# A state-space layer beside a gated feed-forward: another product first, parameters as rows, centring on ScalarE

## The chip, the core and the metric

The kernel runs on one NeuronCore of a Trainium2 chip. Its engines are TensorE (PE, matrix products into PSUM), VectorE (DVE), ScalarE (ACT), GpSimd (POOL) and SyncE (SP, whose queue issues most DMAs). Each has its own instruction stream, and they meet through semaphores. The metric is device time in microseconds (us) of one launch. All times in this text are us unless marked otherwise.

## The reference

```python
def _layernorm(x, axis=-1, eps=1e-5):
    m = jnp.mean(x, axis=axis, keepdims=True)
    v = jnp.var(x, axis=axis, keepdims=True)
    return (x - m) / jnp.sqrt(v + eps)

def _A_ref(x, Lambda_re, Lambda_im, B_re, B_im, C_re, C_im, log_dt, Dskip):
    Lam = Lambda_re + 1j * Lambda_im
    dt = jnp.exp(log_dt)
    Lam_bar = jnp.exp(dt * Lam)
    B_bar = ((Lam_bar - 1.0) / Lam)[:, None] * (B_re + 1j * B_im)
    Bu = jnp.einsum("bld,pd->blp", x + 0j, B_bar)
    # h_t = Lam_bar * h_{t-1} + Bu_t, over the 2048 tokens
    ...
    return 2.0 * jnp.einsum("blp,dp->bld", hseq, C_re + 1j * C_im).real + x * Dskip

def _B_ref(x, w_gate, w_up, w_down):
    return (_gelu(x @ w_gate) * (x @ w_up)) @ w_down

xn = _layernorm(x)
out = x + _A_ref(xn, ...) + _B_ref(xn, ...)
```

There are 2048 tokens of 512 features, 512 complex states, and 1376 hidden columns in the feed-forward. All inputs and the output are bf16.

## The kernel before

**Blocks and tiles.** The tokens are cut into four blocks of 512, each of four tiles of 128. For a block the kernel does the layer norm of its tiles (`LN`), turns them so that features lie on the partitions (`TR`, transposing DMAs; in block 0 `TR_lead`, by TensorE), multiplies by B (`BU`: eight results, real and imaginary part of four groups of 128 states, four matmuls each), rotates, scans and rotates back (`CHAIN`, all on VectorE), multiplies by the gate and up weights (`GU`: eleven column tiles of 128 hidden columns, each a gate and an up product of four matmuls), and makes the output (`DN`: eleven matmuls with w_down and eight with C for each token tile). The factor of B_bar is folded into C (`scale_C`), so B is used as it is loaded, by a transposing DMA (`ld_tr`).

**Evictions.** Results of `BU` are copied out of PSUM by ScalarE (L661), two of block 0 by VectorE (L660). `gu_out` takes the gelu of the gate (L715) and a copy of the up product (L717) on ScalarE and multiplies them on VectorE (L719, hmul), through rings of three buffers. PSUM has eight banks; `next_bank` deals them in turn, so a bank is wanted again eight products later.

**Who sets the order.** The operations are listed with estimated durations. `Sched.schedule` keeps TensorE's and SyncE's order as listed. On VectorE, ScalarE and GpSimd it plays the kernel through with its own estimates, always taking the ready operation whose due time (worked back from TensorE's list, less the operation's `slack`) is earliest, and filling gaps with others. `S.pin` fixes the first operations of an engine in the order given. `Sched.emit` then writes each engine's list with its semaphore waits; the order is fixed when the kernel is built, and an engine waits at the head of its list.

**The lead.** SyncE issues the four tiles of x of block 0, B_re and B_im, then the gate and up weights in four chunks of columns each (`FCH`: 256, 384, 384 and 352 columns; x tiles 4 to 7 after the second chunk). ScalarE issues the three parameter vectors (log_dt, Lambda_im, Lambda_re), element by element onto 128 partitions (L465). TensorE first multiplies zeros (L768, 12 matmuls of 512 columns). Tiles 0 to 2 get their mean and variance by bn_stats and bn_aggr on VectorE (L512, L513), tile 3 by sums on ScalarE (`sums`, L517 to L521). The square root is a power on GpSimd (L542; for a whole block L571), the reciprocal and the centring are on VectorE (L544, L527). Each tile is turned by TensorE (L556, four transposes) and copied by ScalarE (L559, "evT"). While tiles come in, TensorE does the B product for tiles 0 and 1 in pieces of 128 columns in four banks; after the last tile it does what is left of the eight B results.

```python
        S.pin(evT0, t1, evT1, t2, evT2, evT3, t3)
        sint, cost, warm, dtab = tables()
        S.pin(*dtab)
        ev = []
        for k in range(8):
            lead_mm((k,), 2 if k < 4 else 0, 4)
            ev.append(bu_out(0, combos[k][0], combos[k][1], k, "scalar" if k < 6 else "vector"))
        S.pin(*ev[0:6], sint, cost, warm)
        S.pin(*ev[6:8])
```

Here t1 and t2 are the exponentials of the parameters (`decay`, L592 and L595), t3 the sine of 16 small columns (L601), sint and cost the sine tables that the rotations need (L611, L612, from fractions that VectorE makes, L605 to L609). `warm` loads the gelu table before the first gelu (L614).

**After the lead** the order on TensorE is: column tiles 0 to 10 of block 0, B product 1, column tiles of block 1, B product 2, output of block 0, column tiles of block 2, B product 3, output of block 1, column tiles of block 3, outputs of blocks 2 and 3. `LN(1)` uses bn_stats on VectorE, `LN(2)` and `LN(3)` use sums on ScalarE and centre on VectorE.

Of the kernel before, what the change touches and what calls it, by code (L numbers as in the profile page):

```python
# [75 lines left out]
class Sched:  # L76
# [58 lines left out]
    def schedule(self):  # L135
# [41 lines left out]
        while nleft:  # L177
            best = None
            for e in ENGINES:
# [29 lines left out]
                if best is None or st < best[0]:  # L209
                    best = (st, op)  # L210
            st, op = best
# [108 lines left out]
D_TINY = 90.0  # L320
def d_act(n, ptr=0): return 100.0 + 0.833 * n + 90.0 * ptr


def build(nc, ins, out):
    with ExitStack() as es:
# [51 lines left out]
        NEGt = [[A.sub(A.sub(NEG_all, "NEG%d" % b, b), "NEG%d_%d" % (b, j), j) for j in range(4)] for b in range(NB)]  # L377
# [14 lines left out]
        RQb, RQt = per_tile("RQ")  # L392
        HALF = A.alloc("HALF", [4], BF16)
# [4 lines left out]
        LDT = A.alloc("LDT", [KP], BF16)  # L398
# [63 lines left out]
        def ld_param(T_, nm, queue="sync"):  # L462
            def f(e):
                with nc.allow_non_contiguous_dma(reason="tiny per-state parameter vectors"):
                    return e.dma_start(T_.ap, ins[nm].rearrange("(s p) -> p s", p=128))  # L465
            return S.dma(f, 1024, writes=[T_], tag="ld_" + nm, queue=queue, issue=530.0, lat=4000.0)

        def ld_tr(dst, nm):
            return S.dma(lambda e: e.dma_start_transpose(dst.ap, ins[nm]), 3.0 * 512 * 1024 * 0.33, writes=[dst], tag="tr_" + nm,
                         issue=1900.0, lat=1000.0)  # L470

        for tt in range(4):
            ld_x(tt, 1)
        S.pin(*[ld_param(T_, nm, "scalar") for T_, nm in ((LDT, "A_log_dt"), (LIM, "A_Lambda_im"), (LRE, "A_Lambda_re"))])
        ld_tr(BBT[0], "A_B_re")
        ld_tr(BBT[1], "A_B_im")
        for ci in range(4):
            ld_w(WG, WGc, ins["B_w_gate"], ci)
            ld_w(WU, WUc, ins["B_w_up"], ci)
            if ci == 1:  # L480
                ld_x(4, 4)

        def late_loads():
            ld_x(8, 4)
# [23 lines left out]
        GATE = {"gelu": [], "last_gelu": None}  # L508

        def stats(tt):  # L510
            b, j = divmod(tt, 4)
            return [V(lambda e: e.bn_stats(ST[tt].ap, X[tt].ap), 640, [X[tt]], [ST[tt]], "bnst"),  # L512
                    V(lambda e: e.bn_aggr(MVt[b][j].ap, ST[tt].ap), 100, [ST[tt]], [MVt[b][j]], "bnag")]  # L513
# [16 lines left out]
        def LN_lead():  # L530
            st = [stats(tt) for tt in range(3)]
            a3 = sums(3)
            S.pin(*a3)
            ve, rq, ln = [], [], []
            for tt in range(4):
                if tt < 3:
                    ve.append(V(lambda e, tt=tt: e.tensor_scalar(VEt[0][tt].ap, MVt[0][tt].ap[:, 1:2], EPS_BF16, None, ALU.add),
                                D_TINY, [MVt[0][tt]], [VEt[0][tt]], "ve"))
                else:
                    ve.append(V(lambda e, tt=tt: e.tensor_scalar(VEt[0][tt].ap, SSQt[0][tt].ap, 1.0 / D, EPS_BF16, ALU.mult, ALU.add),  # L540
                                D_TINY, [SSQt[0][tt]], [VEt[0][tt]], "ve"))
# [3 lines left out]
                ln.append(center(tt, tt == 3))  # L545
            S.pin(*st[0], ve[0], *st[1], ve[1], rq[0], ln[0], *st[2], ve[2], rq[1], ln[1], ve[3], rq[2], ln[2], rq[3], ln[3])

        def TR_lead(tt):
            bank, half = 6 + tt % 2, tt // 2
            part = bank_part(bank, 1024 * half, 1024 * half + 1024)  # L550
            pt = PSH[bank][:, 512 * half:512 * half + 512]

            def f(e):
                ins_ = None
                for dk in range(KD):
                    ins_ = e.transpose(pt[:, 128 * dk:128 * dk + 128], XN[tt].ap[:, 128 * dk:128 * (dk + 1)], IDN.ap)  # L556
                return ins_
            PE(f, 400, [XN[tt], IDN], [part], "T0")
            return ACT(lambda e: e.activation(XNT[0].ap[:, :, 128 * tt:128 * tt + 128],  # L559
                                              pt.rearrange("p (k t) -> p k t", k=KD), ACTF.Copy),  # L560
                       d_act(512), [part], [XNTt[tt]], "evT")

        def LN(b, on_act=True):
            for tt in range(4 * b, 4 * b + 4):
                sums(tt) if on_act else stats(tt)
            if on_act:
                V(lambda e: e.tensor_scalar(VBb[b].ap, SSQb[b].ap, 1.0 / D, None, ALU.mult), D_TINY, [SSQb[b]], [VBb[b]], "vb")
# [313 lines left out]
```

## Time and profile before

| | |
|---|---|
| times of three runs | 184.75, 184.6, 183.53 us; median 184.6 |
| profiled execution: own time, span | 183.76 us, 182.0 us |
| granted TensorE clock, mean | 0.999 |
| busy PE / DVE / ACT / POOL | 174.4 / 163.4 / 95.6 / 9.2 us |
| DMA moved | 12.38 MB |

The span runs from the first to the last instruction of one profiled execution. A busy share is a mean over the whole span. In the chain view each row names what the end waited for at that time; in the timeline each row is a group of like instructions: start, duration, engine, line, operation, and in brackets how long the engine had stood idle and what ended that. "PEld" is a weight load, "SPq" and "ACTq" are DMA issues.

### The profile page before, as it was taken

To read this page: it belongs to the slowest core of one execution; us is meant where nothing else is said; L and a number is where in the kernel's file an instruction comes from. 1 tells how busy PE (TensorE), PEld (TensorE's weight loads), DVE (VectorE), ACT (ScalarE), POOL (GpSimd) and SP (SyncE) were. 2 spreads that over 40 slices of the span, in tenths; PEclk is the share of its full clock that TensorE was granted. 3 is DMA by queue.
4 is the path that set the end of the run, shared out by engine and by line. 5 is a ranking of instruction groups with operands and counts; after the bars stand their busy time and mean duration, and the time that the engine had idled before them with its cause. 6 is when DMAs were issued, how large, how long until landed. Compare 5 with 4: busy or idle time off the path is not lost.

```text
span 182.0 us, 2379 instructions
## 1 busy us (share of the span) xinstructions
PE 174.4 (96%) x848; PEld 83.3 (46%) x863; DVE 163.4 (90%) x269; ACT 95.6 (53%) x184; POOL 9.2 (5%) x13
## 2 busy tenths in 40 slices
PE   7399999999999999999999999999999999999994
PEld 2184444444444444444444444444444444444463
DVE  4799989999999999979999999998999999999431
ACT  2589996899999999600766774000567720000000
POOL 2400320000020000040000000000000000000000
PEclk9999999999999999999999999999999999999999
DMA  4999414997003100002330000001100000002021
GB/s 93 229 273 361 132 29 98 359 237 198 0 0 77 38 4 0 0 0 86 87 63 2 0 0 0 0 4 58 58 0 0 0 4 0 0 29 86 0 88 31
DMA packets 26827, 12.38 MB, mean 68 GB/s; under 512 B 16992, under 2 KB 26816, under 8 KB 26816
## 3 DMA queue, kind: packets, MB, share of 16 engines
q1 hardware_dynamic: 25232, 12.23, 25.8%
q10 hardware_dynamic: 1584, 0.00, 0.5%
q8 instruction: 7, 0.11, 0.3%
q14 instruction: 4, 0.03, 0.1%
HBM read 6.46 MB, written 2.10 MB: 47 GB/s over the span
## 4 chain that ended last, share of the span: by engine, by line
PE 93%; DMA 2%; ACT 2%; issue 1%; SPq 1%; DVE 0%
PE PS L708 42%; PE PS L742 21%; PE PS L652 15%; PE PS L753 15%; DMA arena<-in_A_x_dram 2%; SPq L451 1%; ACT arena L559 1%; ACT arena L521 0%; ACT arena L517 0%; PE PS L556 0%; DVE arena L760 0%; ACT arena L519 0%; ACT arena L592 0%
## 5 line engine op out<-in xcount | busy, mean ns | idle before, releaser
L708 PE MATMUL PS<-arena 128*128 128x512 bf16 (+1 forms) x345 | 76.3, 379 | 0.4
L708 PEld LDWEIGHTS PS<-arena 128*128 128x128 bf16 (+1 forms) x352 | 35.2, 100 | 40.8
L715 ACT ACTIVATE arena<-PS 128x512 bf16<-128x512 f32 (+1 forms) x44 | 26.4, 600 | 34.9 <-PE PS L708 17.2
L742 PE MATMUL PS<-arena 128*128 128x512 bf16 (+3 forms) x184 | 38.9, 366 | 0.2
L690 DVE TENSOR_TENSOR_SCAN arena<-arena 128x512 bf16<-128x512 f32 x32 | 38.8, 1252 | 0.0
L652 PE MATMUL PS<-arena 128*128 128x512 bf16 (+2 forms) x157 | 28.7, 336 | 2.9 <-ACT arena L592 2.5
L717 ACT ACTIVATE arena<-PS 128x512 bf16<-128x512 f32 (+1 forms) x44 | 26.3, 597 | 7.0 <-PE PS L708 7.0
L753 PE MATMUL PS<-arena 128*128 128x512 bf16 (+1 forms) x134 | 28.5, 366 | 0.1
L742 PEld LDWEIGHTS PS<-arena 128*128 128x128 bf16 (+1 forms) x187 | 18.3, 98 | 20.0
L652 PEld LDWEIGHTS PS<-arena 128*128 128x128 bf16 x160 | 14.3, 98 | 16.3 <-DMA arena<-in_A_B_re_dram 2.6
L753 PEld LDWEIGHTS PS<-arena 128*128 128x128 bf16 x136 | 13.2, 97 | 14.4
L719 DVE TENSOR_TENSOR arena<-arena 128x512 bf16<-128x512 bf16 (+1 forms) x44 | 17.8, 417 | 1.8 <-ACT arena L717 1.3
L661 ACT ACTIVATE arena<-PS 128x512 bf16<-128x512 f32 x30 | 17.0, 597 | 2.9 <-PE PS L652 2.9
L679 DVE TENSOR_TENSOR arena<-arena 128x4096 bf16<-128x4096 bf16 x8 | 18.3, 2288 | 0.1
L680 DVE TENSOR_TENSOR arena<-arena 128x4096 bf16<-128x4096 bf16 x8 | 18.3, 2282 | 0.0
L760 DVE TENSOR_TENSOR arena<-PS,arena 128x512 bf16<-128x512 f32 (+1 forms) x17 | 10.9, 652 | 8.0 <-PE PS L753 7.8
L730 DVE TENSOR_TENSOR arena<-arena 128x512 f32<-128x512 bf16 x16 | 10.8, 689 | 0.4
L681 DVE TENSOR_TENSOR arena<-arena 128x2048 bf16<-128x2048 bf16 x8 | 9.8, 1223 | 0.2
L571 POOL TENSOR_TENSOR arena<-arena 128x4 bf16<-128x4 bf16 x3 | 6.0, 2005 | 64.4 <-DVE arena L570 64.4
L517 ACT ACTIVATE arena<-arena 128x512 bf16<-128x512 bf16 x9 | 5.6, 627 | 3.2 <-DMA arena<-in_A_x_dram 3.1
L521 ACT ACTIVATE arena<-arena 128x512 bf16<-128x512 bf16 x9 | 6.5, 717 | 0.1
L729 DVE TENSOR_TENSOR arena<-arena 128x512 bf16<-128x512 bf16 x16 | 6.4, 417 | 0.0
(61 smaller groups left out, 76.3 us busy)
## 6 DMA issues: line engine op xcount, KB each, us to landing
out_dram<-arena SPq DMA_DIRECT2D x15, 128.0 KB, 1.7
arena<-in_A_x_dram SPq DMA_DIRECT2D x3, 512.0 KB, 5.4
arena<-in_B_w_down_dram SPq DMA_DIRECT2D x1, 1280.0 KB, 7.1
arena<-in_B_w_gate_dram SPq DMA_DIRECT2D x2, 384.0 KB, 5.6
arena<-in_B_w_up_dram SPq DMA_DIRECT2D x2, 384.0 KB, 6.1
arena<-in_A_x_dram SPq DMA_DIRECT2D x4, 128.0 KB, 2.9
arena<-in_B_w_gate_dram SPq DMA_DIRECT2D x1, 352.0 KB, 7.7
arena<-in_B_w_up_dram SPq DMA_DIRECT2D x1, 352.0 KB, 7.6
```

The costliest lines, as they stand in the source:

```text
L652: ins_ = e.matmul(PS[bank][:, c0:c1], BBT[c].ap[:, dk, 128 * s:128 * (s + 1)], XNT[b].ap[:, dk, c0:c1], start=(dk == 0), stop=(dk == KD - 1))
L661: return ACT(lambda e: e.activation(ss.ap, PS[bank][:, :], ACTF.Copy), d_act(512), [BANK[bank]], [ss], "evBu")
L679: V(lambda e: e.tensor_tensor(TB.ap, ssb.ap, sin4, ALU.mult), d_dve_tt2x(4096), [ssb, SINT], [TB], tag)
L680: V(lambda e: e.tensor_tensor(TA.ap, ssb.ap, cos4, ALU.mult), d_dve_tt2x(4096), [ssb, COST], [TA], tag)
L690: V(lambda e, g=g, rb=rb, init=init: e.tensor_tensor_scan(g.ap, rb, g.ap, init, ALU.mult, ALU.add), d_dve_scan(512), [g, PA[RRr]] + ([CARc ...
L708: ins_ = e.matmul(PS[bank][0:m, :], W.ap[:, dk, 128 * ft:128 * ft + m], XNT[b].ap[:, dk, :], start=(dk == 0), stop=(dk == KD - 1))
L715: GATE["last_gelu"] = ACT(lambda e: e.activation(GG[kk].ap[0:m, :], PS[bg][0:m, :], ACTF.Gelu_apprx_tanh), d_act(512), [BANK[bg]], [GG[kk] ...
L717: ACT(lambda e: e.activation(UPB[kk].ap[0:m, :], PS[bu][0:m, :], ACTF.Copy), d_act(512), [BANK[bu]], [UPB[kk]], "evU")
L719: V(lambda e: e.tensor_tensor(HTt[k2][ft].ap[0:m, :], GG[kk].ap[0:m, :], UPB[kk].ap[0:m, :], ALU.mult), d_dve_tt2x(512), [GG[kk], UPB[kk]] ...
L742: ins_ = e.matmul(o_, HTt[k2][ft].ap[0:m, tok], WD.ap[0:m, ft, c0:c1], start=(ft == 0), stop=False)
L753: ins_ = e.matmul(o_, SSc[k3][s][c].ap[:, tok], CT[c][s].ap[:, c0:c1], start=False, stop=(s == KP - 1 and c == 1))
L760: V(lambda e, o_=o_, ko=ko: e.tensor_tensor(OUTB[ko].ap[:, c0:c1], o_, XD[ko].ap[:, c0:c1], ALU.add), d_dve_1x(c1 - c0), [part, XD[ko]], [ ...
```

## The change

The order in block 0 becomes: gate and up products of the first three column tiles, in six banks, for token tiles 0 and 1 in pieces of 128 columns, then for tiles 2 and 3 in one piece of 256; then the whole B product of block 0, all eight results copied out by VectorE; then column tiles 3 to 10. The first two gate and up chunks are loaded right behind the four tiles of x, B after them, and x tiles 8 to 11 earlier. The parameters are loaded as four rows of 128 (256 bytes each) and turned by TensorE between two parts of the warm-up (`TR_par`, into PSUM); ScalarE reads them there, and the product dt * Lambda_re becomes the scale of four exponentials. The gelu table is loaded a first time after the exponentials and again after the sine tables; the gelu and the up copy of the third column tile come behind that. Tile 3 gets its statistics on VectorE like the others. Blocks 2 and 3 are centred on ScalarE, with a scale and a bias per token. Some due times get a slack of 4000 ns, the estimate of a transposing load of B or C grows, and the B product goes through the real results first.

```diff
         def ld_param(T_, nm, queue="sync"):
-            def f(e):
-                with nc.allow_non_contiguous_dma(reason="tiny per-state parameter vectors"):
-                    return e.dma_start(T_.ap, ins[nm].rearrange("(s p) -> p s", p=128))
-            return S.dma(f, 1024, writes=[T_], tag="ld_" + nm, queue=queue, issue=530.0, lat=4000.0)
+            return S.dma(lambda e: e.dma_start(T_.ap[0:KP, :], ins[nm].rearrange("(s p) -> s p", p=128)), 1024,
+                         writes=[T_], tag="ld_" + nm, queue=queue, lat=2300.0)
...
+        S.pin(*[ld_param(T_, nm, "scalar") for T_, nm in ((PRM[0], "A_log_dt"), (PRM[1], "A_Lambda_re"), (PRM[2], "A_Lambda_im"))])
         for tt in range(4):
             ld_x(tt, 1)
-        S.pin(*[ld_param(T_, nm, "scalar") for T_, nm in ((LDT, "A_log_dt"), (LIM, "A_Lambda_im"), (LRE, "A_Lambda_re"))])
+        ld_gu(0)
+        ld_gu(1)
         ld_tr(BBT[0], "A_B_re")
         ld_tr(BBT[1], "A_B_im")
-        for ci in range(4):
-            ld_w(WG, WGc, ins["B_w_gate"], ci)
-            ld_w(WU, WUc, ins["B_w_up"], ci)
-            if ci == 1:
-                ld_x(4, 4)
+        ld_x(4, 4)
+        ld_gu(2)
+        ld_gu(3)
+        ld_x(8, 4)
...
         def stats(tt):
             b, j = divmod(tt, 4)
-            return [V(lambda e: e.bn_stats(ST[tt].ap, X[tt].ap), 640, [X[tt]], [ST[tt]], "bnst"),
-                    V(lambda e: e.bn_aggr(MVt[b][j].ap, ST[tt].ap), 100, [ST[tt]], [MVt[b][j]], "bnag")]
+            return [V(lambda e: e.bn_stats(ST[tt].ap, X[tt].ap), 640, [X[tt]], [ST[tt]], "bnst", slack=4000.0),
+                    V(lambda e: e.bn_aggr(MVt[b][j].ap, ST[tt].ap), 100, [ST[tt]], [MVt[b][j]], "bnag", slack=4000.0)]
...
         def LN_lead():
-            st = [stats(tt) for tt in range(3)]
-            a3 = sums(3)
-            S.pin(*a3)
+            st = [stats(tt) for tt in range(4)]
...
-            S.pin(*st[0], ve[0], *st[1], ve[1], rq[0], ln[0], *st[2], ve[2], rq[1], ln[1], ve[3], rq[2], ln[2], rq[3], ln[3])
+            S.pin(*st[0], ve[0], *st[1], ve[1], rq[0], ln[0], *st[2], ve[2], rq[1], ln[1], *st[3], ve[3], rq[2], ln[2])
+            return rq[3], ln[3]
...
+        PPB = (5, 5, 4)
+        PP = [PSH[PPB[i]][:, KP * i:KP * (i + 1)] for i in range(3)]
+
+        def TR_par(i):
+            PE(lambda e: e.transpose(PP[i], PRM[i].ap[0:KP, :], IDN.ap[0:KP, 0:KP]), 100, [PRM[i], IDN], [BANK[PPB[i]]], "Tp")
...
+            if on_act:
+                V(lambda e: e.tensor_tensor(NRQb[b].ap, NEGb[b].ap, RQb[b].ap, ALU.mult), D_TINY, [NEGb[b], RQb[b]], [NRQb[b]], "nrq")
+            for j in range(4):
+                tt = 4 * b + j
+                if on_act:
+                    ACT(lambda e, j=j, tt=tt: e.activation(XN[tt].ap, X[tt].ap, ACTF.Identity, bias=NRQb[b].ap[:, j:j + 1],
+                                                           scale=RQb[b].ap[:, j:j + 1]),
+                        d_act(512, 1), [X[tt], NRQb[b], RQb[b]], [XN[tt]], "ln")
+                else:
+                    center(tt, False)
...
         def decay():
+            exps = [ACT(lambda e: e.activation(DTB.ap, PP[0], ACTF.Exp), 200, [BANK[5]], [DTB], "exp_dt")]
+            for s in range(KP):
+                exps.append(ACT(lambda e, s=s: e.activation(PA[RRr].ap[:, s:s + 1], PP[1][:, s:s + 1], ACTF.Exp,
+                                                            scale=DTB.ap[:, s:s + 1]),
+                                200, [BANK[5], DTB], [A.sub(PA[RRr], "RR_%d" % s, s)], "exp_a"))
+            c = [ACT(lambda e: e.activation(LRE.ap, PP[1], ACTF.Copy), 200, [BANK[5]], [LRE], "par"),
+                 ACT(lambda e: e.activation(LIM.ap, PP[2], ACTF.Copy), 200, [BANK[4]], [LIM], "par")]
...
-        def BU(b):
-            for s in range(KP):
-                for c in range(2):
-                    bank = next_bank()
-                    bu_mm(b, s, c, bank, 0, 512, [XNT[b]])
-                    bu_out(b, s, c, bank)
+        def BU(b, eng="scalar", banks=None):
+            combos = [(s, c) for c in range(2) for s in range(KP)]
+            for i, (s, c) in enumerate(combos):
+                bank = banks[i] if banks else next_bank()
+                bu_mm(b, s, c, bank, 0, 512, [XNT[b]])
+                bu_out(b, s, c, bank, eng)
...
+        def lead_mm(pairs, t0, t1):
+            for k in pairs:
+                gu_mm(0, k, 2 * k, 2 * k + 1, t0, t1)
+
+        def preload(tag):
+            return ACT(lambda e: e.activation(DUM.ap[:, 1:2], DUM.ap[:, 0:1], ACTF.Gelu_apprx_tanh), 1500, [DUM], [DUM], tag)
+
+        rq3, ln3 = LN_lead()
+        warm_pe(6)
+        TR_par(0)
+        TR_par(1)
+        warm_pe(5)
+        TR_par(2)
+        exps, cps, dec, t3 = decay()
+        gelu0 = preload("ld_gelu")
+        GATE["gelu"] = [gelu0]
+        evT = [TR_lead(0)]
+        lead_mm((0,), 0, 1)
+        evT.append(TR_lead(1))
+        lead_mm((1, 2), 0, 1)
+        evT.append(TR_lead(2))
         lead_mm((0, 1), 1, 2)
+        evT.append(TR_lead(3))
+        lead_mm((2,), 1, 2)
+        S.pin(*exps, gelu0, evT[0], *cps, *evT[1:])
+        S.pin(rq3, ln3, *dec)
+        late = []
+        for k in range(3):
+            lead_mm((k,), 2, 4)
+            g, u, h = gu_out(0, k, 2 * k, 2 * k + 1)
+            (S.pin if k < 2 else lambda *o: late.extend(o))(g, u)
+        sint, cost, gelu1, dtab = tables()
+        GATE["gelu"] = [gelu1]
+        S.pin(*dtab)
+        S.pin(t3, sint, cost, gelu1, *late)
+        BU(0, "vector", (6, 7, 0, 1, 2, 3, 6, 7))
+        rstate["n"] = 0
         factor()
         CHAIN(0)
         LN(1, False)
         TR(1)
         late_loads()
-        GU(0, range(0, 8))
+        GU(0, range(3, 8))
```

## The prediction

> **What bounds the kernel now.** I read the busy shares first, then the chain that ended last, then the waits, then the timeline of the first 36 us engine by engine.
>
> ```profile
> PE 174.4 (96%) x848; PEld 83.3 (46%) x863; DVE 163.4 (90%) x269; ACT 95.6 (53%) x184; POOL 9.2 (5%) x13
> PE 93%; DMA 2%; ACT 2%; issue 1%; SPq 1%; DVE 0%
> ```
>
> TensorE (PE) is busy for 96% and holds 93% of the chain: the end is set by when its stream starts and whether it is ever stopped. The chain in order of time shows the start:
>
> ```profile
> 8.02 0.48 ACT arena L559
> 8.50 0.10 ACT arena L592
> ...
> 8.64 0.61 PE PS L652 x8
> ...
> 11.70 1.92 PE PS L652 x16
> ...
> 179.53 0.42 DVE arena L760
> ```
>
> From 11.70 to 179.51 us PE streams without a stop (167.8 us). Before 11.70 it did 32 matmuls of 128 columns (0.61 us per eight) and 16 transposes, and stood still once:
>
> ```profile
> PEld PS L652 <- DMA arena<-in_A_B_re_dram: 2.6, 1, 2.6
> PE PS L652 <- ACT arena L592: 2.5, 1, 2.5
> ```
>
> That is 6.19 to 8.64: the copy of transposed tile 0 (evT0, L559) queues on ScalarE behind the sums of tile 3, which wait for its DMA, and B_re's transposing load lands only then. Everything the change can win lies ahead of 11.70, plus nothing in the tail (179.5 to 182.0), which it leaves alone.
>
> **Part 1, lead order.** After the change 48 matmuls of 128 columns stand ahead of the bulk instead of 32 (three pairs, two tiles, eight matmuls each): 6144 columns instead of 4096. The bulk is shorter by 2048 columns, four 512-column matmuls at 0.216 us (L742, 38 in 8.21 us): **0.86 us**. The start of the bulk follows step by step:
> - VectorE's (DVE) row of steps to the last centring gains one bn_stats and bn_aggr (0.73 and 0.22 start to start, 3.11 to 4.06) but they fill its old wait at 7.3 to 8.05. Adding starts: stats 3 at 7.18, centring 2 at 8.38, square root 3 on GpSimd (0.56) done 8.92, centring 3 at 9.15 to 9.56, exactly where it is now.
> - ScalarE: parameter row loads are three issues as before (0.46 each). The transposes of the parameters wait for the first two loads. The nearest row is a 128 KB tile of x, 2.4 us from issue to landing, so 3.6 for the second; the element-wise loads took 2.9 to 4.2, so 5.4 at the latest. Six cold warm-up matmuls (weight loads every 0.43 us) end at 3.75, so the wait costs nothing or up to 1.6; behind it on PE stand the second warm-up and transpose 0, behind them on ScalarE evT0. I take 3.8, the x row being nearer for a row load. Then five exponentials (0.2 first, 0.1 apart) to 4.7, the gelu preload 1.28 + 0.2 to 6.2, evT0 6.2 to 6.8 (it starts at 7.92 now).
> - PE from 6.85: eight matmuls 0.61, transpose 1 0.22, sixteen 1.22, transpose 2 0.22, sixteen 1.22, transpose 3 at 10.34 + 0.42, evT3 0.61: bulk at **11.42** if weights are there.
> - Weights: pair 2's up matrix (second chunk) is wanted at 8.6. Now the same 1.28 MB start flowing near 9.9 and the last lands at 15.15 (issue 9.76 + 5.4), 5.25 us. After the four x tiles they can start at 3.6 (issue 2.6 + 1.0 to the first bytes): landing near 8.85. If x's last tile is as late as now (6.19, data about 1 ahead of the landing), 10.4. At the 350 GB/s of 13 to 18 us it is 3.7 plus that 1, so 8.3. I take 8.9, which takes the row of these same four loads: 0.3 of waiting, then 0.31 + 0.22 + 1.22 + 0.42 + 0.61 and the bulk at **11.7**, as now. Bounds 11.42 to 13.2.
>
> So Part 1 is worth 0.86, bounds +1.14 to -0.64.
>
> **The added table load** is the step the profile can price best:
>
> ```profile
> 11.04 0.60 ACT L559 ACTIVATE arena<-PS 128x512 bf16<-128x512 bf16 x1 [0.26 <-PE PS L556]
> ...
> 11.66 1.28 ACT L601 ACT_TABLE_LOAD   x1
> ...
> 12.95 0.21 ACT L601 ACTIVATE arena<-arena 128x16 f32<-128x16 f32 x1
> ```
>
> The load starts 0.02 after the copy ends and the next activation follows at once, so 1.28 is all of it. [...]
>
> The row decides; a load that costs more is a rival below.
>
> **Part 2, B product and its evictions.** 32 matmuls of 512 run after the lead's rest (24 of 256, 0.108 each: 11.7 to 14.3), so 14.3 to 21.2. B_re is issued at 4.85 and B_im behind it; behind a backlog C_re took 8.4 and C_im 5.8 with issues of 5.85 and 2.13, which gives 13.3 and 16.5, wanted at 14.3 and 17.8: nothing, with 1.0 us of cover (each us beyond is a us of PE). All eight evictions go to DVE (0.69 each, two there now): +4.1 us of DVE at 16 to 25. ScalarE evicts pairs 0 and 1 by 14.5, then sine load and tables (1.28 + 0.2 + 1.95 + 2.04), gelu load and then pair 2 at about 21.1 to 22.2. Banks 4 and 5 are wanted again by column tile 5 at 24.7: hidden, 2.5 us of cover. The parameter copies (two of 0.2) stand ahead of evT1, which waits for PE anyway.
>
> **Part 3, what the loaded DVE makes late.** Block 1's centring is next:
>
> ```profile
> 20.77 2.28 DVE L679 TENSOR_TENSOR arena<-arena 128x4096 bf16<-128x4096 bf16 x1
> 20.94 2.99 POOL L571 TENSOR_TENSOR arena<-arena 128x4 bf16<-128x4 bf16 x1 [12.10 <-DVE arena L570]
> ...
> 24.37 0.73 DVE L527 TENSOR_SCALAR arena<-arena 128x512 bf16<-128x512 bf16 x2
> ...
> 24.80 5.14 SPq L579 DMA_TRANSPOSE arena<-arena  x4
> ...
> 36.12 6.85 PE L652 MATMUL PS<-arena 128*128 128x512 bf16 x31
> ```
>
> Four transposing DMAs take 5.14 us of SyncE's (SP) queue and land 2.5 after the issue, so the last lands 6.8 after the first centring: 31.2, 4.9 ahead of B product 1. Six more evictions (0.65 back to back) push the first centring from 24.4 to about 28.4, the last landing to 35.2; PE wants it at 36.12 - 0.86 = 35.26. I take no stop; the cover is gone but for 0.1 us, and from 28.5 on each us is a us of PE. A shorter square root (2.99 beside L679; 1.12 and 1.91 in the other blocks) gives up to 1.9 back. The slack of 4000 puts block 1's stats among the evictions: four bn_stats (2.46) ahead of the fourth eviction make it end near 21.9, wanted at 22.15 (second bank of column tile 3); if x tiles 4 to 7 land after 18.6 that becomes a stop. They land 16.6 now; issued near 11.3 with 3.8 to 6.3 to landing they come at 15.1 to 17.6.
>
> **Part 4, centring of blocks 2 and 3 on ScalarE.** DVE loses eight centrings (four in 1.38) and gains two products of 0.15: -2.5 us, so over the run DVE has about 2.5 more with the tile 3 stats (0.95). ScalarE gains eight at about 0.71 (L521, with a pointer operand) of its 47% idle time; behind them stand gelu and up evictions, which hold banks, and gaps of 0.3 to 0.5 in each column tile take them. Block 3's rotation ends at 159.2 and its product starts at 170.2: 11 us of cover. Block 2's transposes are issued at 54.9 and land at 61.2, wanted at 61.9, 0.7 us of cover; x tiles 8 to 11 now arrive ten us earlier (issued ahead of TR(1) in an idle stretch of SP, 15 to 24.8) and ve/vb are taken early, so I cost it at nothing. If the centrings queued, each late us is a us.
>
> **Sum.** -0.86 +0 +0 +0. The profiled run has a span of 182.0 and took 183.76; it becomes 181.1 and 182.9. The three times are 183.53 to 184.75 with median 184.6; the mean of all four is 184.16, and 184.16 - 0.86 = **183.3 us** is my time. A measurement of this kernel tells about 1% (1.85 us) from no change.
>
> **Rivals.**
> - Lead at its best. Bulk at 11.42 gives 1.14, and the element-wise loads gone (1584 packets, 0.5% of 16 engines' 182 us is 0.9 us of all engines) bring x up to 0.9 earlier, part of which reaches the bulk: 1.5 to 2.0 in all, 182.2. For it: x tile 0 is what DVE waits for at first (1.46 us). Against: evT0 is then held by the preload.
> - DVE backlog, the case on the other side. First centring at 24.4 + 4.0 + 0.65 (x tiles late) + 2.28 (a rotation taken while the square root runs, as at 20.77) = 31.3: last transpose at 38.1, PE stops 2.8 at B product 1, less 0.86: +1.95, 186.1. It begins at a centring later than 28.5, is slower than before from 29.4 and by 1% from 31.2. For: DVE has no idle time from 16 on. Against: due times favour block 1, and the square root may be short.
> - Weights late: landing 9.9 to 10.4, bulk 12.7 to 13.2, +0.1 to +0.6: 184.5. For: loads behind others took 4.0 to 7.7 to land. Against: the element-wise loads that slow x now are gone.
> - The preload costs a second 1.28: evT0 at 7.5, lead 1.28 later, bulk at 13.0, +0.4: 184.6. Against: all three loads here take 1.28 with no gap behind. [...]
>
> **How the numbers follow.** Forecast 0.43 (182.6 to 184.0), best lead 0.18 (faster by over 1%), backlog 0.22 (about at 1% slower and beyond), weights 0.13, preload 0.04 (both within 1%). So faster 0.18, same 0.60, slower 0.22. The low end is the lowest time less the best lead, 183.53 - 1.6 = 181.9; the high end 184.16 + 1.6 = 185.8 takes in most of the backlog.
>
> **What would show it.** Right: evT0 ends before 7, the eight-matmul groups run from about 6.9, the bulk starts at 11.4 to 12, no PE wait above 0.3 after it, first centring of block 1 by 28.5, PE's last matmul near 178.6. Wrong: a PE wait on a weight DMA near 8.6, on a DVE eviction at 21 to 24, or on TR(1) before B product 1; a table load followed by a gap; half-speed matmuls in the lead.

## The result, and the profile after

| | before | after |
|---|---|---|
| median of 13 runs each, on one chip | 184.60 (183.53 to 185.22) | 185.09 (184.59 to 186.74) |
| ratio | | 1.0055, 95% interval 1.0030 to 1.0081 |
| profiled execution: own time, span | 183.76, 182.0 | 184.71, 182.9 |

The change makes the kernel slower by about half a per cent; a gain, to 183.3, had been forecast. TensorE still sets the end. These are the page's busy shares of the kernel after, and its chain that ended last:

```profile
PE 175.6 (96%) x881; PEld 84.2 (46%) x881; DVE 164.8 (90%) x270; ACT 98.7 (54%) x188; POOL 10.9 (6%) x13
PE 91%; DMA 3%; SPq 2%; ACT 1%; issue 0%; DVE 0%
```

TensorE holds 91% of the chain instead of 93%, a transfer has come in with 3%, and GpSimd is busy for 1.7 us more. The chain of the kernel after in order of time (start, duration, what) says where:

```profile
4.24 5.88 DMA arena<-in_B_w_up_dram
...
12.59 2.79 PE PS L725 x24
15.38 6.91 PE PS L669 x32
22.29 12.10 PE PS L725 x56
...
36.84 7.07 PE PS L669 x32
...
180.47 0.43 DVE arena L779
```

The bulk starts at 12.59 (11.70 before), and the stream is broken between 36.1 and 36.84. Before, the chain reached the first bulk matmul through ScalarE's sums of tile 3 and evT0; now it reaches it through the load of the second up chunk. The view of waits of the kernel after, TensorE's rows (total, times, longest), names both:

```profile
PE PS L725 <- DMA arena<-in_B_w_up_dram: 0.8, 1, 0.8
PE PS L669 <- ACT arena L735: 0.7, 1, 0.7
PE PS L725 <- DMA arena<-in_B_w_gate_dram: 0.6, 1, 0.6
```

The middle row is the stop ahead of B product 1. ScalarE is named there because its eviction came last in the profile's events, but the eviction is not what was late: in the run with ScalarE padded (below) the product starts at 35.92, while that eviction runs from 35.91 to 36.50.

**The sum of the pair of profiles.** Bulk later by 0.89; 2048 columns fewer, -0.86; stop at B product 1, +0.89. The stop costs more than the 0.73 us of idle time that the view lists: 32 matmuls take 6.91 in the chain where the stream runs on (at 15.38) and 7.07 behind the stop (at 36.84), so the overlap of 0.16 between one group and the next is lost as well. Together +0.92; the step behind the last matmul starts 0.94 later (180.47 against 179.53), and the spans differ by 0.9. Nothing else on TensorE's stream has moved by more than some hundredths.

**Which execution stands for before.** The runs of the kernel before lie in two groups, 183.53 to 183.70 (five) and 184.60 to 185.22 (eight), with nothing between. The profile shown of before is of the lower group, the median of the upper. Over all the comparisons of this study 81 runs of it have a listed clock: 29 have a mean granted clock of 0.999 or 1.000 and times up to 184.03, 52 have 0.98 to 0.991 and times from 184.45 on. Of the 13 runs after, only two are at 0.991 (186.49 and 186.74); the other eleven have a median of 185.05. So at equal clock the change costs 185.05 - 183.64 = 1.4 us, and about 0.9 of that is hidden in the comparison of the medians, because the low clock is rare in the kernel after. A second profile of the kernel before, the last experiment, shows where the clock was low in one such execution.

### The profile page after: what moved, and what is told of

Read it like the earlier page. It is cut to its first block, busy times and chain, and to the rows that moved or that the text cites. A ratio compares the mean times of both kernels' runs of the same rounds, so it can differ in the third digit from the quotient of the medians.

```text
span 182.9 us, 2423 instructions
## 1 busy us (share of the span) xinstructions
PE 175.6 (96%) x881; PEld 84.2 (46%) x881; DVE 164.8 (90%) x270; ACT 98.7 (54%) x188; POOL 10.9 (6%) x13
## 4 chain that ended last, share of the span: by engine, by line
PE 91%; DMA 3%; SPq 2%; ACT 1%; issue 0%; DVE 0%
PE PS L725 40%; PE PS L761 21%; PE PS L669 15%; PE PS L772 15%; DMA arena<-in_B_w_up_dram 3%; SPq L456 2%; ACT arena L735 1%; ACT arena L560 0%; ACT arena L733 0%; ACT arena L528 0%; PE PS L557 0%; DVE arena L779 0%
## 5 line engine op out<-in xcount | busy, mean ns | idle before, releaser
L725 PE MATMUL PS<-arena 128*128 128x512 bf16 (+3 forms) x400 | 77.9, 353 | 2.8 <-ACT arena L613 1.2
L725 PEld LDWEIGHTS PS<-arena 128*128 128x128 bf16 (+1 forms) x400 | 38.0, 100 | 41.7 <-issue 1.4
L761 PE MATMUL PS<-arena 128*128 128x512 bf16 (+3 forms) x187 | 39.1, 366 | 0.0
L669 PE MATMUL PS<-arena 128*128 128x512 bf16 x128 | 28.3, 379 | 0.7 <-ACT arena L735 0.7
L772 PE MATMUL PS<-arena 128*128 128x512 bf16 (+1 forms) x136 | 28.6, 366 | 0.0
L761 PEld LDWEIGHTS PS<-arena 128*128 128x128 bf16 (+1 forms) x187 | 18.3, 98 | 20.0
L772 PEld LDWEIGHTS PS<-arena 128*128 128x128 bf16 x136 | 13.3, 98 | 14.4
L669 PEld LDWEIGHTS PS<-arena 128*128 128x128 bf16 x128 | 12.5, 98 | 15.8 <-issue 1.2
L678 ACT ACTIVATE arena<-PS 128x512 bf16<-128x512 f32 x24 | 14.1, 592 | 3.4 <-PE PS L669 3.3
L578 POOL TENSOR_TENSOR arena<-arena 128x4 bf16<-128x4 bf16 x3 | 7.8, 2585 | 63.3 <-DVE arena L577 63.3
L585 ACT ACTIVATE arena<-arena 128x512 bf16<-128x512 bf16 x8 | 6.1, 802 | 3.7 <-DVE arena L581 3.7
L519 DVE BATCH_NORM_STATS2 arena<-arena 128x6 f32<-128x512 bf16 x8 | 5.2, 682 | 1.2 <-DMA arena<-in_A_x_dram 1.2
```

The lines of the kernel that those rows point to most:

```text
L669: ins_ = e.matmul(PS[bank][:, c0:c1], BBT[c].ap[:, dk, 128 * s:128 * (s + 1)], XNT[b].ap[:, dk, c0:c1], start=(dk == 0), stop=(dk == KD - 1))
L678: return ACT(lambda e: e.activation(ss.ap, PS[bank][:, :], ACTF.Copy), d_act(512), [BANK[bank]], [ss], "evBu")
L725: ins_ = e.matmul(PS[bank][0:m, c0:c1], W.ap[:, dk, 128 * ft:128 * ft + m], XNT[b].ap[:, dk, c0:c1], start=(dk == 0), stop=(dk == KD - 1))
L761: ins_ = e.matmul(o_, HTt[k2][ft].ap[0:m, tok], WD.ap[0:m, ft, c0:c1], start=(ft == 0), stop=False)
L772: ins_ = e.matmul(o_, SSc[k3][s][c].ap[:, tok], CT[c][s].ap[:, c0:c1], start=False, stop=(s == KP - 1 and c == 1))
```

## The experiments

Theory A for the late bulk: the second up chunk lands late because B_re's transposing load is issued 0.55 behind it and shares the DMA engines. Rival: it is late by the queue of the loads ahead of it (four tiles of x and the first chunk). Theory for the stop: block 1's square root stands still beside VectorE, so that its centring and the transposes come late; theory D: a packet that brings instructions delays the fourth transpose. All edits are made to the kernel after, except in the last two. A letter means the same thing only within one expectation: theory A of the late bulk is called theory C where B is held to 9.63.

| kernel | median | ratio to before, 95% | at full clock, against before at full clock | bulk from | first centring of block 1 | stop at B product 1 |
|---|---|---|---|---|---|---|
| after | 185.09 | 1.0055 (1.0030 to 1.0081) | +1.4 | 12.59 | 29.13 | 0.73 |
| first chunk of 384 | 183.66 | 0.9965 (0.9933 to 0.9998) | 0.0 | 11.37 | 27.94 | 0.69 |
| early root | 183.95 | 0.9985 (0.9951 to 1.0019) | +0.2 | 12.85 | 26.13 | none |
| both | 182.68 | 0.9926 (0.9890 to 0.9962) | -1.0 | 11.40 | 24.69 | none |
| centring on VectorE | 184.86 | 1.0031 (1.0003 to 1.0059) | +1.2 | 12.60 | 29.13 | 0.65 |
| B held to 9.63 | 183.55 | 0.9967 (0.9940 to 0.9994) | -0.2 | 12.08 | 29.89 | none |
| VectorE padded | 184.85 | 1.0030 (1.0005 to 1.0056) | +1.1 | 12.94 | 29.48 | 0.77 |
| ScalarE padded | 184.03 | 0.9970 (0.9948 to 0.9993) | +0.3 | 12.36 | 28.90 | none |
| B held to 7.19 | 184.60 | 1.0005 (0.9972 to 1.0039) | +1.1 | 12.40 | 28.94 | 0.79 |
| before, rows alone | 183.08 | 0.9940 (0.9906 to 0.9973) | -0.7 | 10.77 | 23.44 | none |

The fourth column is the difference of two medians, of the runs with a mean granted clock of 0.999 or 1.000 (8 to 12 of each kernel; of before 5 beside the kernel after, and 13, 12 and 4 on the chips of the three batches that follow). The last three columns are from one profile each; the stop is the idle time that the profile lists. Five of these kernels load the lead's data in the same order (after, early root, centring on VectorE, both padded ones): in their profiles the second up chunk lands at 9.88 to 10.47 and the bulk starts at 12.36 to 12.94. That is the scatter from one profile to another.

### A first chunk of 384 columns

```diff
-        FCH = [(0, 256), (256, 640), (640, 1024), (1024, F)]
+        FCH = [(0, 384), (384, 640), (640, 1024), (1024, F)]
```

> Only the column chunks change: 384, 256, 384, 352 instead of 256, 384, 384, 352, so that the weights of all three lead pairs are the first two loads (768 KB instead of 1280 KB before pair 2 can start). Theory A (the lead loses 1.2 us to weights that land late, and TR(1) loses 0.7 more to the loaded VectorE): the second load lands near 7.5, no PE wait at 8.5 to 10.2, bulk starts at 11.5 to 11.8 instead of 12.59; VectorE's evictions follow PE, so the stop at B product 1 stays between 0 and 0.9; time 184.2 (0.9 below the changed kernel). Theory B (the lead does not matter because block 1's centring sets the start of B product 1): bulk earlier, but the stop grows from 0.73 to 1.6 and the time stays at 185.1.

Three column tiles need 384 columns. Cut so, the lead waits for no second chunk: the up chunk lands at 7.78, and TensorE's row in the timeline is

```profile
7.82 0.40 PE L725 MATMUL PS<-arena 128*128 128x128 bf16 x4 [0.26 <-DMA arena<-in_B_w_up_dram]
```

It waits 0.26 for the chunk, and the bulk starts at 11.37, 1.22 earlier and well outside the scatter. The stop is still there and has not grown, so theory B is out. 1.4 us are gained at the median, 0.5 more than I expected: the whole late start was the second chunk's.

### The early root

```diff
-                V(lambda e: e.tensor_copy(VBb[b].ap, MV[b].ap[:, :, 1]), D_TINY, [MV[b]], [VBb[b]], "vb", slack=4000.0)
-            V(lambda e: e.tensor_scalar(VEb[b].ap, VBb[b].ap, EPS_BF16, None, ALU.add), D_TINY, [VBb[b]], [VEb[b]], "ve", slack=4000.0)
+                V(lambda e: e.tensor_copy(VBb[b].ap, MV[b].ap[:, :, 1]), D_TINY, [MV[b]], [VBb[b]], "vb", slack=12000.0)
+            V(lambda e: e.tensor_scalar(VEb[b].ap, VBb[b].ap, EPS_BF16, None, ALU.add), D_TINY, [VBb[b]], [VEb[b]], "ve", slack=4000.0 if on_act else 12000.0)
```

> Only the due times of block 1's two small variance steps change (slack 12000 instead of 4000), so that they stand right behind the statistics and the square root on GpSimd runs while VectorE copies B results out of PSUM, not beside products of bf16 tiles. Theory A: the root starts near 22 instead of 24.9 and takes under 3 us instead of 3.99, first centring of block 1 by 26.5 instead of 29.1, transposes landed by 33.5, the 0.73 us stop before B product 1 is gone, time 184.4; the lead is as before (bulk 12.59). Rival (the stop comes from the fourth transposing DMA landing 0.7 later than the others, beside the w_down load): still a stop of about 0.7, only earlier issues, time 185.1.

Two tiny VectorE steps are moved ahead in its list. These are GpSimd's and VectorE's rows around the root in the timeline of the kernel after:

```profile
24.89 3.99 POOL L578 TENSOR_TENSOR arena<-arena 128x4 bf16<-128x4 bf16 x1 [16.22 <-DVE arena L577]
...
24.71 1.09 DVE L737 TENSOR_TENSOR arena<-arena 128x512 bf16<-128x512 bf16 x3
25.72 2.29 DVE L696 TENSOR_TENSOR arena<-arena 128x4096 bf16<-128x4096 bf16 x1
28.91 0.18 DVE L579 RECIPROCAL arena<-arena 128x4 f32<-128x4 bf16 x1 [0.91 <-POOL arena L578]
29.13 1.38 DVE L534 TENSOR_SCALAR arena<-arena 128x512 bf16<-128x512 bf16 x4
```

and with the early root:

```profile
22.44 1.01 POOL L578 TENSOR_TENSOR arena<-arena 128x4 bf16<-128x4 bf16 x1 [13.72 <-DVE arena L577]
...
22.27 3.08 DVE L677 CAST arena<-PS 128x512 bf16<-128x512 f32 x5
```

The same 128 x 4 power takes 3.99 us beside two kinds of bf16 product on VectorE and ends 0.87 after the 2.29-us rotation (25.72 + 2.29 = 28.01, the root's end 28.88); beside copies out of PSUM it takes 1.01. I read the other 3.0 as time in which it stands still; that is my estimate from these rows, no view shows a stop inside an instruction. VectorE stands too, 0.91, waiting for it. The neighbours alone do not decide it, though: with B held to 9.63 the root starts 0.84 ahead of the same rotation, behind the same products (here 0.83), and takes 1.12; what makes that difference is open. With the early root the first centring comes 3.0 earlier and TensorE does not stop. The time falls by 1.1 where 0.7 was expected; the stop was worth 0.89 (above), and in this profile the bulk is 0.26 later than in the kernel after (12.85).

### Both

> The first chunk of 384 and the early square root together. Theory A: the two losses add, bulk at 11.5 to 11.8 and no stop at B product 1: 185.1 - 0.9 - 0.7 = 183.5, below the kernel before (184.6) by 0.6%. Theory B or the rival of the early root: 184.2 to 184.4, one of the two gains only.

The two edits together: bulk from 11.40, no stop, 182.68, the best of all kernels here. The ratio to before is 0.9926 (0.9890 to 0.9962), the gain over the kernel after 2.4 us. Between the profiles it is 2.1 (spans of 182.9 and 180.8), which is the bulk's 1.19 and the stop's 0.89; the profiled run of the kernel after is 0.4 below its median, and that is the rest.

### Centring on VectorE

```diff
-                if on_act:
-                    ACT(lambda e, j=j, tt=tt: e.activation(XN[tt].ap, X[tt].ap, ACTF.Identity, bias=NRQb[b].ap[:, j:j + 1],
-                                                           scale=RQb[b].ap[:, j:j + 1]),
-                        d_act(512, 1), [X[tt], NRQb[b], RQb[b]], [XN[tt]], "ln")
-                else:
-                    center(tt, False)
+                center(tt, on_act)
```

> The changed kernel with the centring of blocks 2 and 3 back on VectorE (part 4 undone). Theory A: nothing waits for it either way (transposes of block 2 land over 3 us ahead), 185.1 within 0.3; the stop at B product 1 stays 0.7. Rival (ScalarE's added 6.4 us of centring disturbs the evictions): 184.6 or less.

Blocks 2 and 3 centred on VectorE again: 184.86, bulk and stop as they were. VectorE is busy 2.3 us more and ScalarE 5.4 less, and the end does not notice: the move to ScalarE is worth nothing either way, within 0.3.

### B held behind the second up chunk

```diff
-        ld_gu(1)
-        ld_tr(BBT[0], "A_B_re")
+        up1 = ld_gu(1)
+        ld_tr(BBT[0], "A_B_re", after=[up1])
```

> The changed kernel in which the transposing load of B_re is issued only when the second up chunk has landed. Theory C (the second chunk, 768 KB, lands at 9.0 and 10.1 because B_re's short packets run beside it: 200 GB/s at 6 to 8 us where 300 to 350 stood before): the second up chunk lands at 8.5 to 9.0 instead of 10.1, bulk at 11.5 to 11.8 instead of 12.59, time 184.2 as with the first chunk of 384. Rival (the sixteen DMA engines give the weights no more in this stretch anyway, 1.8 MB at 250 GB/s): lands at 9.8 to 10.2, bulk 12.5, time 185.1 or a little more because B comes later.

The chain of this kernel in order of time:

```profile
4.24 5.37 DMA arena<-in_B_w_up_dram
9.61 0.02 issue
9.63 6.69 DMA arena<-in_A_B_re_dram
...
16.36 3.84 PE PS L669 x17
```

With no transposing load beside it the second up chunk still takes 5.37, 0.51 less than in the kernel after: 9.61, between the 8.5 to 9.0 of the theory and the 9.8 to 10.2 of its rival, and 0.3 below the lowest of the five profiles with the old order. So B_re's load is, by this one profile, about 0.5 of the 1.2 us by which 10.1 misses the 8.9 of the prediction; the rest is not B_re's. Nor do B_re's short packets slow the weights at 6 to 8: in the kernel after, the DMA view counts 4, 11, 182 and 490 packets under 512 B in the four microseconds from 6 on, so they begin at 8. How B_re's load acts on the weights before that is not shown.

In this profile the B product then waits 1.49 for B_re. The profiled run took 184.98, though, and the eleven others 183.21 to 183.91; what B_re did in those no profile shows. If it stopped none of them, a bulk 0.51 earlier and no stop of 0.89 (there is none in this profile: the root takes 1.12 and the instruction packet comes at 40) make 183.7 of 185.05, my estimate.

### B held behind the first up chunk

```diff
-        ld_gu(0)
+        up0 = ld_gu(0)
         ld_gu(1)
-        ld_tr(BBT[0], "A_B_re")
+        ld_tr(BBT[0], "A_B_re", after=[up0])
```

> As the changed kernel, but the issue of B_re waits for the landing of the first up chunk (6.44 there) instead of following the issue of the second at 4.79; no other line changes. Where the lateness of the second up chunk (issue 4.24, landing 10.1) comes from its bytes sharing the DMA engines with B_re's transposing load (theory A): about 1.6 us more of the rate of 300 GB/s for the weights, the landing at 9.1 to 9.7, the bulk at 11.6 to 12.2, B_re there near 13.5, ahead of the 14.4 at which it is wanted, and 0.4 to 1.0 less span than the 182.9 of the changed kernel where the wait at B product 1 (0.73) stays. Rival: the chunk is late by the queue of the loads ahead of it (x and the first chunk): landing at 10.1 and bulk at 12.6 as before, and a time within 0.3 us of 185.1. Second rival, as in the run that held B_re back to 9.63: B_re lands later than 14.4 and gives back what the bulk won.

B_re issued at 7.19 instead of 4.79: the chunk lands at 9.93, the bulk starts at 12.40, and the time is 184.60. Both are within the scatter of the profiles that leave B_re where it was; theory A's landing of 9.1 to 9.7 did not come. Moving B out of the way by this much was not the remedy; asking for the columns that are needed in the first request was.

### VectorE padded, ScalarE padded

```diff
+        PADS = ring(A.alloc("PAD", [20], F32), "PAD", 20)
+        S.pin(*[V(lambda e, p=p: e.memset(p.ap, 0.0), 10, [], [p], "pad") for p in PADS])
```

```diff
-        S.pin(*exps, gelu0, evT[0], *cps, *evT[1:])
+        PADS = ring(A.alloc("PAD", [16], F32), "PAD", 16)
+        pads = [ACT(lambda e, p=p: e.activation(p.ap, HPI.ap, ACTF.Copy), 80, [HPI], [p], "pad") for p in PADS]
+        S.pin(*exps, gelu0, evT[0], *cps, evT[1], *pads, *evT[2:])
```

> The changed kernel with 20 tiny memsets on VectorE in its idle time before the first tile of x (1.7 to 2.9 us). They move any loading of instructions for VectorE 20 instructions earlier in its work. Theory D (the fourth transposing DMA of block 1 lands 3.2 instead of 2.5 us after its issue because a packet of the instruction queue q14 stands on one DMA engine at 34 to 36 us; the packet belongs to VectorE): the packet moves to before 33 us, the fourth lands in 2.5, the stop at B product 1 falls from 0.73 to 0.1 or less, time 184.4. If the packet is ScalarE's, or if the stop comes from late centring alone: stop 0.7 as before, time 185.1.

> The changed kernel with 16 tiny copies on ScalarE behind the second eviction of the lead, where it waits for PE (8.6 to 10.8 us). Theory D with the packet being ScalarE's: the q14 packet leaves the stretch 34 to 36 us, the fourth transposing DMA lands in 2.5, the stop at B product 1 falls to 0.1 or less, time 184.4. If it is VectorE's or the centring alone: stop 0.7, time 185.1.

Four transposing DMAs carry block 1 to its B product. Three of them land 2.4 to 2.5 after their issue in the kernel after, the fourth, issued at 33.43, 3.2 after it. From the DMA view of the kernel after between 33.4 and 37 us (queue, kind: packets, MB, share; then an issue with its us to landing):

```profile
q14 instruction: 1, 0.01, 0.6%
...
arena<-arena SPq DMA_TRANSPOSE x1, 3.2
```

A packet that brings instructions passes at 35 to 36. Twenty more instructions on VectorE leave it there and the stop with it (0.77). Sixteen more on ScalarE move it to 29 to 30, and the DMA view from 33.2 to 36.8 and TensorE's row in the timeline become:

```profile
arena<-arena SPq DMA_TRANSPOSE x1, 2.5
```

```profile
35.92 2.32 PE L669 MATMUL PS<-arena 128*128 128x512 bf16 x10
```

No idle time is listed before B product 1 any more, although the root takes 3.99 and the first centring comes at 28.90, 16.54 behind the start of the bulk as in the kernel after. The time falls to 184.03 although ScalarE does more. A little of the stop is left: the product starts 0.2 after the fourth transpose has landed (33.21 + 2.5 and 35.92; in the kernel after 33.43 + 3.2 and 36.84), and a stream that runs on would have started it 0.16 before the 35.87 at which the column tile ends. So of the stop of 0.89 some 0.2 is the late root, which takes the cover away, and 0.7 is the packet of ScalarE's instructions.

The other profiles agree. In five of the nine kernels with the change (after, first chunk, centring on VectorE, VectorE padded, B held to 7.19) the packet passes 1.6 to 1.7 behind the issue of the fourth transpose, which then takes 3.1 to 3.2, and TensorE stops; in the other four it passes at another time, the fourth takes 2.5, and no stop is listed. The w_down load, the rival of the early root, is issued 1.3 behind the fourth transpose in both profiles shown here (34.73 and 34.52), so it is not the cause.

### Before, with the parameters as rows alone

```diff
-        S.pin(*[ld_param(T_, nm, "scalar") for T_, nm in ((LDT, "A_log_dt"), (LIM, "A_Lambda_im"), (LRE, "A_Lambda_re"))])
+        S.pin(*[ld_param(T_, nm, "scalar") for T_, nm in ((PRM[0], "A_log_dt"), (PRM[1], "A_Lambda_re"), (PRM[2], "A_Lambda_im"))])
...
-            t1 = ACT(lambda e: e.activation(DTB.ap, LDT.ap, ACTF.Exp), 200, [LDT], [DTB], "exp_dt")
+            t1 = [ACT(lambda e: e.activation(DTB.ap, PP[0], ACTF.Exp), 200, [BANK[5]], [DTB], "exp_dt"),
+                  ACT(lambda e: e.activation(LRE.ap, PP[1], ACTF.Copy), 200, [BANK[5]], [LRE], "par"),
+                  ACT(lambda e: e.activation(LIM.ap, PP[2], ACTF.Copy), 200, [BANK[4]], [LIM], "par")]
```

> The kernel before with one part of the change alone: parameters loaded as rows and turned by TensorE, order of products as before. Theory A: the 1536 element-wise packets no longer stand beside x, so x tile 3 lands near 4.5 instead of 6.19, ScalarE's sums of tile 3 begin that much earlier, tile 0 is copied by 6.9 instead of 8.5, and PE starts B products when B_re lands (7 to 8.2): bulk at 11.0 to 11.6 instead of 11.70, time 0.1 to 0.7 below the kernel before. Rival (the centring of tile 3, which ends at 9.56 by VectorE's own work, sets the bulk): bulk 11.6 to 11.7, no change.

The kernel before, with only the row loads and the three transposes of the change (`ld_param` and `TR_par` as in the change, called behind the warm-up). In the chain of before the load of x's last tile took 4.07; here the chain has

```profile
2.20 3.03 DMA arena<-in_A_x_dram
```

and the timeline, evT0 and the first pieces of the bulk:

```profile
6.97 0.60 ACT L558 ACTIVATE arena<-PS 128x512 bf16<-128x512 bf16 x1
...
10.77 2.57 PE L659 MATMUL PS<-arena 128*128 128x256 bf16 x19 [0.24 <-ACT arena L558]
```

The last tile of x lands 1.0 earlier (5.2; 4.5 expected), evT0 and the bulk follow by 0.95 and 0.93. It is the 1584 packets of the element-wise loads, now 24, that had held x back. This one part of the change makes the kernel 0.6% faster (0.9940, 0.9906 to 0.9973), 0.7 us at full clock: what it wins, the rest of the change spends.

### Before, a second profile

> The kernel before, unchanged, with a second profile. Its times lie in two groups, near 183.6 and near 184.8 us; the first profile is of the lower group (183.76). Theory A: the 1.1 us come from the lead (the element-wise parameter loads delay a tile of x by more or by less), so that a profile of the upper group would have its bulk start 1 us later than 11.70 and all else alike. Rival: from the tail or from outside the span, the bulk at 11.7 and the span at 182.0 with 2.8 us around it. A profile of the lower group again would leave it open.

This profile is of the upper group (184.93, span 183.1). The bulk starts at 12.86 instead of 11.70 and everything behind it is 1.16 later. TensorE in a table of windows of this execution (window, its length, TensorE busy with instructions, granted clock, DMA share, GB/s) and its timeline:

```profile
7.00:8.00 1.00, 0.00 (x0) 1.00 0.95 173
8.00:9.00 1.00, 0.63 (x8) 0.76 1.07 227
9.00:10.00 1.00, 1.00 (x12) 0.50 1.02 214
10.00:11.00 1.00, 1.00 (x12) 0.50 0.92 215
11.00:12.00 1.00, 1.00 (x12) 0.53 0.96 261
```

```profile
8.37 0.91 PE L652 MATMUL PS<-arena 128*128 128x128 bf16 x8 [2.18 <-ACT arena L592]
9.08 0.63 PE L556 MATMUL PS<-arena 128*128 128x128 bf16 x4
```

After the wait of 2.18 us for evT0 the clock falls to half at 8.5 and is back at 11.9, so that in the chain eight lead matmuls take 0.85 to 0.91 instead of at most 0.62, and four transposes 0.43 instead of 0.22. That the bulk would be 1 us later was expected; that the parameter loads delay x by more is wrong for this execution, as x's last tile lands earlier here (2.13 + 3.79 = 5.92) than in the first profile (6.19). So in this execution a stretch of 3.4 us at half clock follows an idle time of 2.2. In the first profile the same wait was longer, 2.46, and the clock stayed at full (1.00 in each microsecond from 7 to 12), so the length of the wait alone does not decide. What does, and why 52 of 81 executions have the low clock and 29 have not, no run here shows. The ten other kernels wait 0.8 to 1.3 in the lead and have the low clock in 13 of 117 runs, two of them with the rows alone, whose wait is 0.78. None of these 13 was profiled, so what lowers the clock there is open.

## Why the prediction was wrong, point by point

**What bounds the kernel: half right.** The start of the bulk was rightly read as the place where anything could be won. But the profile read was of the lower group, and I did not ask what made the published times fall into two groups 1 us apart; I averaged them to 184.16. The wait of 2.5 us that I named as what the change could win is, in the one execution profiled at the low clock, followed by the half clock (0.50 for 3.4 us). The change cuts the wait to 1.2 (TensorE resumes at 7.18), and the low clock falls from 52 of 81 runs to 2 of 13. That is some 0.9 at the median that the prediction had nowhere; that the shorter wait is the reason is likely, not shown. At equal clock -0.86 was forecast and +1.4 came; that the medians differ by only 0.5 is luck.

**Part 1, the lead before the weights: right.** These rows of the kernel after stand against evT0 at 6.2 and a table load of 1.28 with no gap behind it:

```profile
5.05 1.28 ACT L797 ACT_TABLE_LOAD   x1
6.34 0.20 ACT L797 ACTIVATE arena<-arena 128x1 f32<-128x1 f32 x1
6.45 0.58 ACT L560 ACTIVATE arena<-PS 128x512 bf16<-128x512 bf16 x1
```

evT0 came 0.25 late and TensorE resumed 0.33 late (7.18; 6.85 predicted), both hidden by the wait for the weights; centring 3 came at 8.90 (9.15 predicted), and the load costs 1.28 and nothing behind it (5.05 + 1.28 = 6.33, the next activation at 6.34): the rival of a second 1.28 is out.

**Part 1, the weights: the step that failed.** I had the last of the two chunks landing at 8.9, from the 5.25 us that the same 1.28 MB had taken later on; the bound was 10.4, and it landed at 10.1. The timeline of the kernel after has the two waits and the start:

```profile
9.01 0.40 PE L725 MATMUL PS<-arena 128*128 128x128 bf16 x4 [0.55 <-DMA arena<-in_B_w_gate_dram]
...
10.16 0.40 PE L725 MATMUL PS<-arena 128*128 128x128 bf16 x4 [0.76 <-DMA arena<-in_B_w_up_dram]
...
12.59 2.79 PE L725 MATMUL PS<-arena 128*128 128x256 bf16 x24 [0.24 <-ACT arena L560]
```

This is the rival "Weights late", to which I gave 0.13: it names the landing (9.9 to 10.4) and puts the bulk at 12.7 to 13.2, a little beyond the 12.59 that came. My argument against it, that the loads which slow x are gone, was true (x tiles land 2.1 to 2.3 after issue now), but the weights did not gain from it. The 1.28 MB in 5.25 us, some 245 GB/s, were exceeded from 5 to 6 us (316 GB/s) and missed from 6 to 8 (203 and 224). B_re's load behind them accounts for about 0.5 us of the landing; why the rate is 248 GB/s between 6 and 7 with B held back too, and the remaining 0.7, are open. The term beside it was right: the 24 pieces of 256 columns take 2.79 with the overlap of 0.16 at their end, so 0.110 each where I used 0.108.

**Part 2, B product and evictions: right.** B_re landed 7.3 after its issue (12.1; 13.3 put down) and B_im at 14.3, ahead of need; the B product follows without a gap (15.38 to 22.29), and no bank is late.

**Part 3, the loaded VectorE: right in kind, wrong by 0.9 in what it costs.** I took the first centring at 28.4, the last landing 6.8 behind it, and a cover of 0.1 us, and booked that as no stop. The centring came at 29.13, but so did the bulk later: counted from the bulk it is 16.54, against 16.7 in the forecast. The late bulk is not to blame either, for it moves the need as much; with the first chunk of 384 the bulk starts at 11.37 and the stop is 0.69. What tipped it was the fourth transpose, 3.2 from issue to landing where I used 2.5 for all four: 0.7. The other 0.2 was a cover that was never there. The row of before that I read, 36.12, has 31 of the product's 32 matmuls and takes 6.85, where 32 behind a stop take 7.07; the first one, missing from the trace, puts the start at 35.9, so the need was 0.2 earlier than I had it, and the product that waits starts 0.2 behind the landing (36.84 against 33.43 + 3.2), which I had left out. With the centring 0.16 early that makes 0.1 + 0.16 - 0.2 - 0.2, some 0.15 short, near the 0.2 that ScalarE padded shows.

That the centring came where I had put it, counted from the bulk, is luck in part. I had let a shorter square root give up to 1.9 back; it came 1.0 longer than the 2.99 of before, and the steps ahead of it were shorter than I had them by a little more. That root is what keeps the centring so late: the early root brings it to 13.3 behind the bulk. I had used the term ("a rotation taken while the square root runs") in the backlog rival alone. A cover of 0.1 us should not have been booked as no stop.

**Part 4: right.** Centring on ScalarE costs and brings nothing that can be measured (185.09, and 184.86 with it back on VectorE).

**The rivals.** What came is "Weights late" with a small piece of "DVE backlog" (0.89 instead of 2.8), 0.9 over the profile of before. Two of the signs that the prediction lists for being wrong came with them: a wait on a weight DMA (at 9.01 and 10.16), and one on the transposes of block 1 before B product 1. "Lead at its best" was real in its second half: the row loads are worth 0.93 of bulk start in the old order, where evT0 hangs on x's last tile. In the new order evT0 hangs on the gelu table, as I had said against it.

## What to carry to other kernels

When a change moves an early product to other operands, cut the first request of each load to what the lead needs (here 384 columns instead of 256: 1.2 us of bulk start), and take the landing of a load in the lead from its queue, not from a later stretch of the trace. Before a profile is read, see in which group of the kernel's times it falls and compare its granted clock with that of the others: a wait in TensorE's lead may cost its own length and then, as in the one execution profiled, half of the clock for 3.4 us behind it. Hold a difference between single profiles against the scatter of profiles that should agree. Where the cover of a step comes out at a tenth of a microsecond, list what can stretch each of its links (a neighbour on VectorE, an instruction packet) and book the likelier one.

## What the runs showed of the hardware

- A small GpSimd power that starts 0.83 to 0.84 us ahead of a VectorE product of two 128 x 4096 bf16 tiles: 3.99 or 4.00 us in six profiles, ending some 0.9 after that product, and 1.12 in a seventh; beside copies out of PSUM 1.01.
- A packet of ScalarE's instructions 1.6 to 1.7 us behind the issue of a transposing DMA: 3.1 to 3.2 from issue to landing in five profiles instead of 2.5 in the other four; 16 instructions more on ScalarE moved the packet by 6 us, and the stop of TensorE went.
- After 2.2 us without a matmul in the lead the granted clock stood at 0.50 for 3.4 us, 1.16 us of time, in one profile; in another, after 2.46 us, it stayed at full. In 52 of 81 runs of that kernel the mean granted clock was 0.98 to 0.991.
- Beside element-wise loads of three vectors of 512 bf16 values (1584 packets) the last 128 KB tile of x landed at 6.19 and at 5.92 us in two profiles, beside row loads of the same vectors (24 packets) at 5.2 in one.
